# PSUM given out as three pairs of banks, each read by one VectorE operation, in a mixer kernel on one core

## The chip, the cores and the metric

The kernel runs on one core of a Trainium2 chip. The metric is the device time of one execution in microseconds, the median of several runs. TensorE (PE) multiplies, with its weight loads shown as PEld; VectorE (DVE) and ScalarE (ACT) read TensorE's results out of PSUM; GpSimd (POOL) and SyncE (SP) mostly issue DMAs. [...]

## What is computed

```python
# x: (8, 4096, 192), softmax weights over 7 taps for each of 8 heads
w = softmax(weight)                                    # (8 heads, 7 taps)
x = causal convolution of x with w along the sequence  # (8, 4096, 192)
xt = x.transpose(0, 2, 1)
h = np.maximum(xt @ w_tok1, 0.0) @ w_tok2              # mixes the 4096 tokens through 256
u = x + h.transpose(0, 2, 1)
h2 = np.maximum(u @ w_ch1, 0.0) @ w_ch2                # mixes the 192 channels through 1536
return (u + h2).astype(np.float32)
```

Weights arrive as float64, are decoded on the chip, and split into a high and a low fp32r part, so that most products are made of three matmuls: high by high, high by low, low by high.

## The kernel before

The eight batches are worked in five groups: 0, 1, then 2 and 3, 4 and 5, 6 and 7 (`GROUPS`). For each group stage 1 makes the convolution (taps on VectorE, line 718) and the first token product (line 821 for one batch, 825 to 827 for two) into two PSUM banks of their own, `ps_a`. Then the tokens are walked in eight tiles of 512 (`q`), and each tile is 4 blocks of 128 tokens (`j`, `TJ = 4`).

For a tile and a batch the order on TensorE is this. `channel1` (line 1154) multiplies the tile with `w_ch1`: six turns `p`, each of 18 matmuls into two banks; ScalarE writes the ReLU `hh` of each bank (line 1212) and VectorE the remainder `hl` (line 1213), which also is the last read of the bank. In the last batch of a group's tile, `mix2` then makes the next tile's second token product (lines 980 and 981 for one batch, 983 to 985 for two), a bank for each `j`, and VectorE adds it to `u` (lines 989, 990, or 1000 with a VectorE transpose on line 1001). `channel2` (lines 1247 and 1248) multiplies by `w_ch2`, a bank for each `j`, and VectorE makes two adds for each `j` into `osb` (lines 1253 and 1254). It is called for the first half (`j` = 0, 1) and for the second (`j` = 2, 3). Between the halves the next tile is turned so that channels lie on partitions. In the first group, and in the first turns of the second, that is `transposed()`: eight TensorE transposes into two banks (line 1040), copies on ScalarE and a subtraction on VectorE (line 1043). In later turns it is done by VectorE's 32x32 transposes, 16 DMAs (`blocks_sent`, line 1071) and copies (`parted`, lines 1100 to 1107), under channel2. From the third group on the tiles of the first batch use `channel2_halves` (line 1230), two banks for each `j`, and in some turns `mix2_halves` (line 1015).

All of these take their banks from one pool, `ps_x`, of six buffers of a bank each. The pool gives them out in turn: the seventh request gets the first bank again, and its first matmul waits until all that read or wrote that buffer are done.

Convolution, decoding and the first token product of the coming groups run in the background. `Background` holds queues of items, each with a cost in ns. After each piece of foreground work `bg.fg(pe, dve, after)` advances a planned TensorE clock and pops items until the planned VectorE clock is `after` ahead of TensorE's, then charges `dve` for the foreground's own VectorE work. So these numbers set in which order VectorE's instructions stand. `pop` lets the VectorE clock lag at most 3 us behind before it counts an item.

Of the kernel before, what the change touches and what calls it, by code (L numbers as in the profile page):

```python
# [139 lines left out]
def conv_mixer_kernel(ctx: ExitStack, tc: tile.TileContext, x, weight, w_tok1, w_tok2, w_ch1, w_ch2, out):  # L140
# [6 lines left out]
    P = 128  # L147
# [239 lines left out]
    def mix1_done(gi, accs):  # L387
        n = len(GROUPS[gi]) * D
        for kc in range(KC):
            a = accs[kc][:, :n]  # L390
            nc.scalar.activation(out=h1[:, kc, 0, :n], in_=a, func=AF.Relu)
            nc.vector.scalar_tensor_tensor(
                out=h1[:, kc, 1, :n], in0=a, scalar=0.0, in1=f32(h1[:, kc, 0, :n]), op0=ALU.max, op1=ALU.subtract
            )
# [15 lines left out]
    def stage1_first(pe, p0, p1, pd, late, load_u, load_next, after, thirds, hooks):  # L410
# [90 lines left out]
        def keep_busy(n):  # L501
            ps = ps_x.tile([P, TT], F32, name="ps_x")
            for k in range(n):
                nc.tensor.transpose(out=ps[:, k % TJ * P:(k % TJ + 1) * P], in_=ident, identity=ident)

        def make_band(between):
# [16 lines left out]
            for hs in halves:  # L523
                if hs.start:
                    between()
                ps = ps_x.tile([P, P // BC, H2, BC], F32, name="ps_x")
# [3 lines left out]
                ps = ps_x.tile([P, 2, 2, BC], F32, name="ps_x")  # L530
# [7 lines left out]
        def conv_mm(m):  # L538
# [424 lines left out]
    def mix2(gi, q, t2, u, turned=None):  # L963
# [9 lines left out]
        for j in range(TJ):  # L973
            ps = ps_x.tile([P, TT], F32, name="ps_x")
# [11 lines left out]
            bg.fg(570 if nb == 1 else 1040, 660 if nb == 1 else 600, 200)  # L986
            if nb == 1:
                two, one = flat(u)[:, j, 0], flat(u)[:, j, 1]
                nc.vector.tensor_tensor(out=one, in0=ps[:, D:2 * D], in1=one, op=ALU.add)
                nc.vector.tensor_tensor(out=two, in0=ps[:, :D], in1=one, op=ALU.add)  # L990
                if turned is not None:
                    nc.vector.transpose(
                        out=by_rows(turned, 1)[:, :, :, j * QB:(j + 1) * QB],
                        in_=two.rearrange("p (c q e) -> p c q e", c=ND, e=QB),
                    )
                    bg.dve += 380
            else:
                uj = u[:, j]
                v = ps[:, :n].rearrange("p (b c d) -> p c b d", b=nb, d=D2)
                nc.vector.tensor_tensor(out=uj, in0=v, in1=uj, op=ALU.add)  # L1000
                nc.vector.transpose(
                    out=by_rows(turned, nb)[:, :, :, j * QB:(j + 1) * QB],
                    in_=uj.rearrange("p c b d -> p c (b d)").rearrange("p c (q e) -> p c q e", e=QB),
                )
                bg.dve += 580

    def mix2_halves(gi, t2, u, turned, j):
        nb = len(GROUPS[gi])
        n = nb * D
        pss = [ps_x.tile([P, TT], F32, name="ps_x") for _ in range(2)]  # L1010
# [9 lines left out]
        uj = u[:, j]  # L1020
        for ps in pss:
            v = ps[:, :n].rearrange("p (b c d) -> p c b d", b=nb, d=D2)
            nc.vector.tensor_tensor(out=uj, in0=v, in1=uj, op=ALU.add)
        nc.vector.transpose(
            out=by_rows(turned, nb)[:, :, :, j * QB:(j + 1) * QB],
            in_=uj.rearrange("p c b d -> p c (b d)").rearrange("p c (q e) -> p c q e", e=QB),
# [5 lines left out]
    def transposed(u):  # L1032
# [4 lines left out]
        for c, (cs, rs) in enumerate(((slice(0, P), slice(0, P)), (slice(P, D), low))):  # L1037
            ps = ps_x.tile([P, TT], F32, name="ps_x")
# [88 lines left out]
    def first_mix(t2, between=None, u=None):  # L1127
        u = first["u"][1] if u is None else u
        for j in range(TJ):
            ps = ps_x.tile([P, TT], F32, name="ps_x")  # L1130
# [5 lines left out]
            bg.fg(650, 350, 200)  # L1136
            two, one = flat(u)[:, j, 0], flat(u)[:, j, 1]
            nc.vector.tensor_tensor(out=two, in0=ps[:, :D], in1=one, op=ALU.add)
# [8 lines left out]
    def channel1_mm(t, p, prods=PRODS, pss=None, last=False):  # L1147

        a, z = pss is None, last or prods[-1] == PRODS[-1]
        pss = pss or [ps_x.tile([P, TT], F32, name="ps_x") for _ in range(2)]  # L1150
        for n, (w, v, c) in enumerate(prods):
            for h, ps in enumerate(pss):
# [375 lines left out]
```

## Time and profile before

| | |
|---|---|
| median of 3 runs | 2005.45 us (2005.21 to 2005.59) |
| the profiled execution | 2005.44 us, span 2003.7 us |
| busy, share of the span | PE 1998.3 us (100%), PEld 1851.7 (92%), DVE 1500.3 (75%), ACT 779.9 (39%), POOL 205.8 (10%) |
| granted TensorE clock | 1.0 |

The span is the time from the first to the last instruction, and 1.7 us lie around it. In the rows of the groups by line, the columns are the line, engine, operation, what it writes and reads with the shapes and the count, then busy us and mean ns of one, then the idle time of the engine ahead of it and what ended it. Rows of the timeline and of the chain begin with the start in us and the length in us. A matmul's end is modelled and matmuls overlap, so their starts are the better clock.

### The profile page before, as it was taken

Reading aid. Unit: us, or ns where it says so; the run is one execution under the profiler, and the core shown is the slowest. Engines: PE = TensorE matmul, PEld = TensorE weight load, DVE = VectorE, ACT = ScalarE, POOL = GpSimd, SP = SyncE. Lnnn points to the kernel's source line nnn. Section 1 sums busy time; section 2 is a strip of 40 time slices with the busy share of each in tenths; the row PEclk is TensorE's granted clock in tenths of the full one; section 3 lists DMA queues with packets and bytes.
Section 4 is the critical chain, followed back from the end, with each engine's and each line's share of the span. In section 5 each row is a group of like instructions: output and inputs, shape, how many; then the busy total and the mean of one; then the engine's idle time right before and its main releaser. Section 6 shows DMA issues by size and latency. Waiting matters only on the chain.

```text
span 2003.7 us, 44785 instructions
## 1 busy us (share of the span) xinstructions
PE 1998.3 (100%) x18652; PEld 1851.7 (92%) x18652; DVE 1500.3 (75%) x2998; ACT 779.9 (39%) x1292; POOL 205.8 (10%) x385
## 2 busy tenths in 40 slices
PE   9999999999999999999999999999999999999999
PEld 9899999999999999998999999999999999999998
DVE  8889989999759998848975789556666666666664
ACT  5777534534343443423433433323233322333322
POOL 0000000011211101111011010101111101011110
PEclk9999999999999999999999999999999999999999
DMA  9947445556465457514664434433223233233310
GB/s 308 317 137 226 151 129 171 177 161 195 159 179 144 134 160 201 158 51 115 165 172 110 126 101 143 136 88 85 78 49 85 72 84 77 71 85 86 85 49 17
DMA packets 270361, 262.21 MB, mean 131 GB/s; under 512 B 189136, under 2 KB 218192, under 8 KB 270160
## 3 DMA queue, kind: packets, MB, share of 16 engines
q1 hardware_dynamic: 248432, 185.27, 32.6%
q0 software_dynamic: 21728, 74.08, 12.1%
q8 instruction: 148, 2.42, 0.5%
q14 instruction: 53, 0.43, 0.1%
HBM read 146.31 MB, written 71.30 MB: 109 GB/s over the span
## 4 chain that ended last, share of the span: by engine, by line
PE 93%; DVE 4%; ACT 1%; DMA 1%; issue 0%; SPq 0%; DVEq 0%; ACTq 0%
PE ps_x L1154 38%; PE ps_x L1230 23%; PE ps_x L1247 12%; PE ps_x L1248 5%; PE ps_x L1015 2%; PE ps_a L825 2%; PE ps_a L826 2%; PE ps_a L827 2%; DVE xc L718 2%; PE ps_a L476 1%; PE ps_x L983 1%; PE ps_x L980 1%; PE ps_x L985 1%; PE ps_x L984 1%; PE ps_a L821 1%; DMA early_raw<-in_moe_w_tok_dram 1%
## 5 line engine op out<-in xcount | busy, mean ns | idle before, releaser
L1212 ACT ACTIVATE hh<-ps_x 128x512 fp32r<-128x512 f32 x744 | 404.0, 596 | 844.1 <-PE ps_x L1154 844.0
L1213 DVE SCALAR_TENSOR_TENSOR hl<-ps_x,hh 128x512 fp32r<-128x512 f32 x744 | 476.9, 685 | 188.1 <-ACT hh L1212 186.8
L1230 PE MATMUL ps_x<-w,hh 64*128 64x384 f32 x3360 | 481.5, 355 | 0.0
L1230 PE MATMUL ps_x<-w,hl 64*128 64x192 f32 x3360 | 423.0, 247 | 0.0
L718 DVE SCALAR_TENSOR_TENSOR xc<-raw,cw,xc 128x384 f32<-128x384 f32 (+1 forms) x768 | 387.9, 561 | 7.8 <-ACT xc L716 7.8
L1247 PE MATMUL ps_x<-w,hh 128*128 128x384 f32 x1284 | 369.6, 359 | 0.0
L1154 PE MATMUL ps_x<-other,w_hi 64*128 64x512 f32 x1296 | 337.4, 388 | 0.0
L1154 PE MATMUL ps_x<-own_hi,w_hi 64*128 64x512 f32 x1440 | 333.3, 392 | 0.5 <-DVE osb L1238 0.3
L1154 PE MATMUL ps_x<-own_hi,w_lo 64*128 64x512 f32 x1440 | 327.3, 387 | 0.0
L1154 PE MATMUL ps_x<-own_lo,w_hi 64*128 64x512 f32 x1440 | 327.0, 387 | 0.0
L1230 PEld LDWEIGHTS ps_x<-w,hl 64*128 64x128 f32 x3360 | 323.6, 188 | 0.9
L1248 PE MATMUL ps_x<-w,hl 128*128 128x192 f32 x1284 | 321.4, 250 | 0.0
L1230 PEld LDWEIGHTS ps_x<-w,hh 64*128 64x128 f32 x3360 | 317.8, 184 | 0.9
L1154 PEld LDWEIGHTS ps_x<-other,w_hi 64*128 64x128 f32 x1296 | 235.5, 184 | 22.9 <-issue 0.4
L1248 PEld LDWEIGHTS ps_x<-w,hl 128*128 128x128 f32 x1284 | 245.1, 191 | 0.0
L1154 PEld LDWEIGHTS ps_x<-own_lo,w_hi 64*128 64x128 f32 x1440 | 218.1, 184 | 25.9 <-ACT own_lo L1046 0.4
L1154 PEld LDWEIGHTS ps_x<-own_hi,w_lo 64*128 64x128 f32 x1440 | 218.2, 184 | 25.8
L1247 PEld LDWEIGHTS ps_x<-w,hh 128*128 128x128 f32 x1284 | 241.1, 188 | 0.4 <-DVE hl L1213 0.4
L1154 PEld LDWEIGHTS ps_x<-own_hi,w_hi 64*128 64x128 f32 x1440 | 212.3, 184 | 31.4 <-issue 4.6
L1154 PE MATMUL ps_x<-other,w_lo 64*128 64x512 f32 x648 | 181.5, 386 | 0.0
L1238 DVE TENSOR_TENSOR osb<-ps_x,osb 128x192 f32<-128x192 f32 x420 | 150.2, 358 | 25.0 <-DVE osb L1238 0.5
L1236 DVE TENSOR_TENSOR osb<-ps_x,u 128x192 f32<-128x192 f32 x140 | 49.8, 355 | 135.8 <-PE ps_x L1230 135.8
(185 smaller groups left out, 2426.3 us busy)
## 6 DMA issues: line engine op xcount, KB each, us to landing
raw<-in_x_dram SPq DMA_DIRECT2D x56, 672.0 KB, 7.4
t<-t2d SPq DMA_DIRECT2D x64, 512.0 KB, 5.5
u<-xcd SPq DMA_DIRECT2D x62, 384.0 KB, 7.4
xcd<-xc POOLq DMA_DIRECT2D x28, 768.0 KB, 8.3
t<-t1p SPq DMA_DIRECT2D x32, 512.0 KB, 4.5
out_dram<-osb POOLq DMA_DIRECT2D x34, 384.0 KB, 3.2
out_dram<-osb SPq DMA_DIRECT2D x29, 384.0 KB, 2.8
t2d<-stage SPq DMA_DIRECT2D x16, 512.0 KB, 4.8
```

Of the source, the lines that this page charges most:

```text
L718: nc.vector.scalar_tensor_tensor(out=dst, in0=src, scalar=cw[:, h, k:k + 1], in1=dst, op0=ALU.mult, op1=ALU.add)
L825: nc.tensor.matmul(out=ps, lhsT=wh, rhs=xh, start=a, stop=False)
L826: nc.tensor.matmul(out=ps, lhsT=wh, rhs=xl, start=False, stop=False)
L827: nc.tensor.matmul(out=ps, lhsT=wl, rhs=xh, start=False, stop=z)
L1154: nc.tensor.matmul(out=ps, lhsT=w1[w][rows, t[h][2][c], p * P:(p + 1) * P], rhs=t[h][v][rows, c], start=a and n == 0, stop=z and n == len( ...
L1212: nc.scalar.activation(out=h["hh", f], in_=ps, func=AF.Relu)
L1213: nc.vector.scalar_tensor_tensor(out=h["hl", f], in0=ps, scalar=0.0, in1=f32(h["hh", f]), op0=ALU.max, op1=ALU.subtract)
L1230: nc.tensor.matmul(out=ps[:, :m], lhsT=h[part, f][ks, ts], rhs=w2[ks, f, :m], start=n == 0 and part == "hh", stop=z and part == "hl",)
L1236: nc.vector.tensor_tensor(out=rows(osb[:, j]), in0=rows(pss[0][:, :D]), in1=tokens(u, i)[:, j], op=ALU.add)
L1238: nc.vector.tensor_tensor(out=osb[:, j], in0=v, in1=osb[:, j], op=ALU.add)
L1247: nc.tensor.matmul(out=ps[:, :2 * D], lhsT=h["hh", f][:, ts], rhs=w2[:, f, :], start=n == 0, stop=False)
L1248: nc.tensor.matmul(out=ps[:, :D], lhsT=h["hl", f][:, ts], rhs=w2[:, f, :D], start=False, stop=z)
```

## The change

The pool becomes three buffers of two banks. `banks()` takes a pair, `bank()` takes a pair and uses the first half only. Where work filled two banks, one VectorE operation now reads both: in `channel1` the remainder of both halves (but for the last `p`, which has one operation for each bank), in `mix2` and `channel2` the adds of two `j`, in `first_mix` and `first_channel2` the same for the first tiles. The transposes on VectorE stay one for each `j`. `mix1_done` writes `h1` in the order of `u`, so that an add over two batches is contiguous, and makes its remainder by batch. `transposed` and `keep_busy` take `bank()`. The charges to the planner change with it: for a pair of `j`, 0 after the first and 1120 after the second in place of 660 each (`mix2` for one batch and `channel2`), 930 in place of 600 each (`mix2` for two), 1250 in place of 1300 in `channel1`.

```diff
-    ps_x = ctx.enter_context(tc.tile_pool(name="ps_x", bufs=6, space=bass.MemoryType.PSUM))
+    ps_x = ctx.enter_context(tc.tile_pool(name="ps_x", bufs=3, space=bass.MemoryType.PSUM))
+    def banks():
+        return ps_x.tile([P, 2, TT], F32, name="ps_x")
+    def bank():
+        return banks()[:, 0]
...
     def mix2(gi, q, t2, u, turned=None):
...
-            ps = ps_x.tile([P, TT], F32, name="ps_x")
+            if j % 2 == 0:
+                pair = banks()
+            ps = pair[:, j % 2]
...
-                nc.vector.tensor_tensor(out=one, in0=ps[:, D:2 * D], in1=one, op=ALU.add)
-                nc.vector.tensor_tensor(out=two, in0=ps[:, :D], in1=one, op=ALU.add)
+                nc.vector.tensor_tensor(out=one, in0=pair[:, :, D:2 * D], in1=one, op=ALU.add)
+                nc.vector.tensor_tensor(out=two, in0=pair[:, :, :D], in1=one, op=ALU.add)
...
-                nc.vector.tensor_tensor(out=uj, in0=v, in1=uj, op=ALU.add)
-                nc.vector.transpose(
+                nc.vector.tensor_tensor(out=uj, in0=pair[:, :, :n], in1=uj, op=ALU.add)
+                for k in range(2):
+                    nc.vector.transpose(
...
     def transposed(u):
...
-            ps = ps_x.tile([P, TT], F32, name="ps_x")
+            ps = bank()
...
     def channel1(t, hold):
...
-            bg.fg(2040 if p else 2400, 1300)
-            for f, ps in pss:
-                nc.scalar.activation(out=h["hh", f], in_=ps, func=AF.Relu)
+            bg.fg(2040 if p else 2400, 1250)
+            hh, hl = parts["hh", p], parts["hl", p]
+            for k in range(2):
+                nc.scalar.activation(out=hh[:, k], in_=pss[:, k], func=AF.Relu)
+            for ks in [slice(0, 1), slice(1, 2)] if p == NP - 1 else [slice(0, 2)]:
                 nc.vector.scalar_tensor_tensor(
-                    out=h["hl", f], in0=ps, scalar=0.0, in1=f32(h["hh", f]), op0=ALU.max, op1=ALU.subtract
+                    out=hl[:, ks], in0=pss[:, ks], scalar=0.0, in1=f32(hh[:, ks]), op0=ALU.max, op1=ALU.subtract
                 )
...
     def channel2(i, h, u, osb, js, at=None):
-        for j in js:
+        pair, last = banks(), js[-1]
+        for k, j in enumerate(js):
...
-            ps = ps_x.tile([P, TT], F32, name="ps_x")
+            ps = pair[:, k]
...
-                    bg.fg(1140, 660 if z else 0, 200)
+                    bg.fg(1140, (0, 660, 1120)[len(js)] if z and j == last else 0, 200)
...
-            nc.vector.tensor_tensor(out=rows(osb[:, j]), in0=rows(ps[:, :D]), in1=tokens(u, i)[:, j], op=ALU.add)
-            nc.vector.tensor_tensor(out=osb[:, j], in0=ps[:, D:2 * D], in1=osb[:, j], op=ALU.add)
+        pair, js = pair[:, :len(js)], slice(js[0], last + 1)
+        nc.vector.tensor_tensor(
+            out=osb[:, js].rearrange("p j (c d) -> p j c d", d=D2),
+            in0=pair[:, :, :D].rearrange("p j (c d) -> p j c d", d=D2), in1=tokens(u, i)[:, js], op=ALU.add,
+        )
+        nc.vector.tensor_tensor(out=osb[:, js], in0=pair[:, :, D:2 * D], in1=osb[:, js], op=ALU.add)
```

Two places show what becomes of the order. The first is TensorE in the third tile of the first group, where channel2's first half ends, the eight transposes follow, and channel2's second half begins. The number behind `ps_x` tells one buffer request from another; the brackets name the engine whose count is waited for. Before, lines 1247 and 1248 are channel2 and 1040 the transposes:

```order
L1247 MATMUL ps_x_1466<-w2_1167,hh8_1222 128x384
L1248 MATMUL ps_x_1466<-w2_1167,hl8_1223 128x192
L1040 MATMUL ps_x_1508<-ident_71,u_1216 128x128 [waits DVE_49,PE_49]
L1040 MATMUL ps_x_1508<-ident_71,u_1216 128x128 [waits DVE_49] x3
L1040 MATMUL ps_x_1515<-ident_71,u_1216 64x128 [waits PE_49]
L1040 MATMUL ps_x_1515<-ident_71,u_1216 64x128 x3
L1247 MATMUL ps_x_1526<-w2_1167,hh0_1218 128x384 [waits PE_49]
L1248 MATMUL ps_x_1526<-w2_1167,hl0_1219 128x192
```

The same place after the change, where channel2 is on lines 1282 and 1283 and the transposes on 1057:

```order
L1282 MATMUL ps_x_1381<-w2_1131,hh8_1186 128x384
L1283 MATMUL ps_x_1381<-w2_1131,hl8_1187 128x192
L1057 MATMUL ps_x_1455<-ident_71,u_1180 128x128 [waits DVE_49,PE_49]
L1057 MATMUL ps_x_1455<-ident_71,u_1180 128x128
L1057 MATMUL ps_x_1455<-ident_71,u_1180 128x128 [waits DVE_49]
L1057 MATMUL ps_x_1455<-ident_71,u_1180 128x128
L1057 MATMUL ps_x_1462<-ident_71,u_1180 64x128 [waits PE_49]
L1057 MATMUL ps_x_1462<-ident_71,u_1180 64x128 x3
L1282 MATMUL ps_x_1473<-w2_1131,hh0_1182 128x384 [waits DVE_49,PE_49]
L1283 MATMUL ps_x_1473<-w2_1131,hl0_1183 128x192
```

The second half's first matmul now also waits for VectorE: by the count it waits for, for the second add that reads `ps_x_1381`, the pair of the first half. The same wait stands in all eight turns that have a whole channel2 around `transposed()`.

The second place is VectorE in the sixth tile of the first group, from mix2's adds (before lines 989 and 990, after 1003 and 1004) to channel2's first-half adds; `xc` is written by taps of the next group's convolution. After the change:

```order
L1246 SCALAR_TENSOR_TENSOR hl8_2345<-ps_x_2475,hh8_2344 128x512
L727 SCALAR_TENSOR_TENSOR xc1_2517<-raw0_2286,cw_70,xc1_2517 128x8x24 [waits DVE_49] x10
L1003 TENSOR_TENSOR u_2338<-ps_x_2503,u_2338 128x2x192 [waits DMAHW4_49,PE_49]
L1004 TENSOR_TENSOR u_2338<-ps_x_2503,u_2338 128x2x192 [waits DVE_49]
L727 SCALAR_TENSOR_TENSOR xc1_2517<-raw0_2286,cw_70,xc1_2517 128x8x24 [waits DVE_49] x6
L1003 TENSOR_TENSOR u_2338<-ps_x_2547,u_2338 128x2x192 [waits PE_49]
L1004 TENSOR_TENSOR u_2338<-ps_x_2547,u_2338 128x2x192 [waits DVE_49]
L727 SCALAR_TENSOR_TENSOR xc1_2517<-raw1_2495,cw_70,xc1_2517 128x8x24 [waits DVE_49] x10
L1289 TENSOR_TENSOR osb_2502<-ps_x_2584,u_1951 128x384 [waits DMASW6_49,PE_49]
L1293 TENSOR_TENSOR osb_2502<-ps_x_2584,osb_2502 128x384 [waits DVE_49]
```

Rows of one or two taps beside these are left out; with them there are 12 taps ahead of the first pair of adds, 8 between the pairs and 18 ahead of line 1289, where before four pairs of shorter adds and channel2's adds for `j` = 0 stood among them. TensorE's mixing matmuls of this turn (line 821 before), which stood inside the half and ahead of, among and behind the transposes, now all stand ahead of channel2's first half.

More of the change, by code (lines that the diff above doesn't have):

```diff
@@ L525, in make_band @@
                     between()
-                ps = ps_x.tile([P, P // BC, H2, BC], F32, name="ps_x")
+                ps = bank().rearrange("p (b h c) -> p b h c", h=H2, c=BC)
                 for b0 in range(P // BC):
@@ L1009, in mix2_halves @@
         n = nb * D
-        pss = [ps_x.tile([P, TT], F32, name="ps_x") for _ in range(2)]
+        pair = banks()
+        pss = pair[:, 0], pair[:, 1]
         prods = [(kc, r, v) for kc in range(KC) for r, v in ((0, 0), (0, 1), (1, 0))]
@@ L1037, in transposed @@
         for c, (cs, rs) in enumerate(((slice(0, P), slice(0, P)), (slice(P, D), low))):
-            ps = ps_x.tile([P, TT], F32, name="ps_x")
+            ps = bank()
             for j in range(TJ):
@@ L1129, in first_mix @@
         for j in range(TJ):
-            ps = ps_x.tile([P, TT], F32, name="ps_x")
+            if j % 2 == 0:
+                pair = banks()
+            ps = pair[:, j % 2]
             for kc in range(KC):
@@ L1135, in first_mix @@
                 )
-            bg.fg(650, 350, 200)
-            two, one = flat(u)[:, j, 0], flat(u)[:, j, 1]
-            nc.vector.tensor_tensor(out=two, in0=ps[:, :D], in1=one, op=ALU.add)
+            bg.fg(650, 560 if j % 2 else 0, 200)
+            if j % 2:
+                two, one = (flat(u)[:, j - 1:j + 1, t] for t in range(2))
+                nc.vector.tensor_tensor(out=two, in0=pair[:, :, :D], in1=one, op=ALU.add)
             if between and j == 0:
@@ L1166, in first_two @@
             done = [channel1_mm(first["abc"][0], p, prods, pss) for p, pss in enumerate(done)]
-        for f, ps in (v for d in done for v in d):
-            nc.scalar.activation(out=first["h"][:, f], in_=ps, func=AF.Relu)
+        for p, pss in enumerate(done):
+            for h in range(2):
+                nc.scalar.activation(out=first["h"][:, p + h * NP], in_=pss[:, h], func=AF.Relu)
         bg.fg(4080, 0)
@@ L1174, in first_channel1 @@
         bg.fg(2040, 0)
-        for f, ps in pss:
-            nc.scalar.activation(out=first["h"][:, f], in_=ps, func=AF.Relu)
+        for h in range(2):
+            nc.scalar.activation(out=first["h"][:, p + h * NP], in_=pss[:, h], func=AF.Relu)
     def first_channel2(u, osb, steps):
@@ L1180, in first_channel2 @@
         n = NF // 3
-        for t, j in steps:
+        for k, (t, j) in enumerate(steps):
             a, z = t == 0, t == 2
-            if a:
-                pss[j] = ps_x.tile([P, TT], F32, name="ps_x")
+            both = j < 2 and (0, 0) in steps and (0, 1) in steps[:2]
+            if a and not (both and j):
+                pss[j] = banks()
+                if both:
+                    pss[1] = pss[0]
+            ps = pss[j][:, j if both else 0]
             for f in range(t * n, (t + 1) * n):
                 nc.tensor.matmul(
-                    out=pss[j][:, :D], lhsT=first["h"][:, f, j * P:(j + 1) * P], rhs=w2f[:, f], start=f == 0,
+                    out=ps[:, :D], lhsT=first["h"][:, f, j * P:(j + 1) * P], rhs=w2f[:, f], start=f == 0,
                     stop=f == NF - 1,
                 )
-            bg.fg(1280, 270 if z else 0, 200)
+            z = z and (j or not both)
+            bg.fg(1280, (560 if both else 270) if z else 0, 200)
             if z:
+                js = slice(0, 2) if both else slice(j, j + 1)
                 nc.vector.tensor_tensor(
-                    out=rows(osb[:, j]), in0=rows(pss[j][:, :D]), in1=tokens(u, 0)[:, j], op=ALU.add
+                    out=osb[:, js].rearrange("p j (c d) -> p j c d", d=D2),
+                    in0=pss[j][:, :js.stop - js.start, :D].rearrange("p j (c d) -> p j c d", d=D2),
+                    in1=tokens(u, 0)[:, js], op=ALU.add,
                 )
@@ L1223, in channel2_halves @@
             ts = slice(j * P, (j + 1) * P)
-            pss = [ps_x.tile([P, TT], F32, name="ps_x") for _ in range(2)]
+            pair = banks()
+            pss = pair[:, 0], pair[:, 1]
             for n, f in enumerate(order):
```

74 lines of the change are left out of this document (42 added, 32 removed).

## The prediction

> **What bounds the kernel now.** First the page's span and busy line for TensorE, with its chain of waits:
>
> ```profile
> span 2003.7 us, 44785 instructions
> ...
> PE 1998.3 (100%) x18652; PEld 1851.7 (92%) x18652; DVE 1500.3 (75%) x2998; ACT 779.9 (39%) x1292; POOL 205.8 (10%) x385
> ...
> PE 93%; DVE 4%; ACT 1%; DMA 1%; issue 0%; SPq 0%; DVEq 0%; ACTq 0%
> ```
>
> TensorE is busy from end to end, and 93% of the chain is TensorE's own work. A matmul's end is modelled, so I asked next for the waits of PE (who waited for whom, us in total, times, longest):
>
> ```profile
> PE ps_x L504 <- POOL ident masks.py:199: 1.4, 1, 1.4
> PE ps_x L1154 <- DVE osb L1238: 0.3, 1, 0.3
> PE ps_a L476 <- ACT xc L569: 0.2, 1, 0.2
> ```
>
> That is 1.9 us. Short waits hide under a modelled end, but show on the weight loads. Those that waited for channel1's VectorE operation (L1213, "who waited for it": us, times):
>
> ```profile
> who waited for it (us, times):
>   PEld ps_x L1154: 2.9, 9
>   PEld ps_x L980: 2.9, 8
> ```
>
> So at most 2.9 + 2.9 = 5.8 us of TensorE's time is owed to VectorE's reads of channel1's banks. VectorE is close to full in only one long stretch, the first group's tiles (columns: length, then busy us of PE, PEld, DVE, ACT, POOL):
>
> ```profile
> 120.00:400.00 280.00, 279.79 (x2117) 263.87 (x2114) 256.22 (x583) 160.07 (x260) 16.59 (x25) 1.00 0.53 169
> ```
>
> 256.22/280 is 92%, yet PE lost 0.21 us there by these rows. The matmuls are the same before and after, so a faster VectorE can give back 5.8 us at most; a new wait on PSUM is paid in full. The question is which waits the new rotation makes.
>
> **Fewer and longer VectorE operations.** Durations by shape:
>
> ```profile
> L1213 DVE SCALAR_TENSOR_TENSOR hl<-ps_x,hh 128x512 fp32r<-128x512 f32 x744 | 476.9, 685 | 188.1 <-ACT hh L1212 186.8
> ...
> L1023 DVE TENSOR_TENSOR u<-ps_x,u 128x384 f32<-128x384 f32 x88 | 48.6, 553 | 4.9 <-DVE u L1023 0.5
> ...
> L1254 DVE TENSOR_TENSOR osb<-ps_x,osb 128x192 f32<-128x192 f32 x107 | 38.3, 358 | 3.7
> L1253 DVE TENSOR_TENSOR osb<-ps_x,u 128x192 f32<-128x192 f32 x107 | 37.8, 354 | 68.5 <-PE ps_x L1248 67.9
> ...
> L205 DVE SCALAR_TENSOR_TENSOR t<-dec_raw,t 128x1024 uint32<-128x1024 uint32 x6 | 7.3, 1222 | 0.1
> ...
> L205 DVE SCALAR_TENSOR_TENSOR w2f<-dec_raw,w2f 128x768 uint32<-128x768 uint32 x3 | 2.9, 958 | 0.1
> ```
>
> A tensor_tensor of 2x192 columns should take what 384 columns take, 0.55 us, in place of two of 0.355; a channel1 operation over 1024 columns 1.22 us (the nearest row, 1024 columns from SBUF) in place of two. VectorE loses some tens of us of work over the run. On the path this is worth nothing by itself: it can only shorten the 5.8 us above.
>
> In channel1 a pair comes free in another order. One pair of a late tile (start, length):
>
> ```profile
> 644.96 0.39 PE L1154 MATMUL ps_x<-other,w_hi 64*128 64x512 f32 x1
> ...
> 645.15 1.09 ACT L1212 ACTIVATE hh<-ps_x 128x512 fp32r<-128x512 f32 x2 [2.57 <-PE ps_x L1154]
> ...
> 645.78 1.29 DVE L1213 SCALAR_TENSOR_TENSOR hl<-ps_x,hh 128x512 fp32r<-128x512 f32 x2
> ```
>
> Before, VectorE starts after the first ReLU (645.78) and is done at 647.07. Now it waits for both (646.24) and ends 1.22 us later, at about 647.5: 0.4 us later than before. Whatever VectorE holds queued behind this operation waits with it, for 0.5 us. TensorE needs those banks three pairs on, after two more pairs of work. From the chain:
>
> ```profile
> 612.58 12.27 PE ps_x L1154 x108
> ```
>
> 12.27/6 = 2.04 us for a pair, so the matmuls that reuse the banks start 4.1 us after the old ones ended (at about 649.1), 1.6 us after the new release. Covered; where VectorE is behind, it is not ReLU that it waits for, and its two operations cost 1.22 in place of 1.29 us. I put this at nothing, and keep 0.5 us in each of ten tiles (5 us) as a bound.
>
> **The new wait.** Six banks gave out one at a time; now three pairs do. In the tiles that use transposed() one turn takes six pairs in channel1, two in mix2, one for channel2's first half, two (one bank of each used) in transposed(), one for the second half. With three buffers, the second half gets the pair that the first half just filled, and must wait for both adds of it (the order in the section before shows that wait). Only the eight transposes stand between. Before, the second half took a bank untouched since long before. This happens in eight turns: the six with q from 2 to 7 of the first group, and two of the second. The first of them, before (PE, then VectorE):
>
> ```profile
> 132.50 0.44 PE L980 MATMUL ps_x<-h,t2s 128*128 128x384 f32 x1
> ...
> 134.88 0.36 PE L1247 MATMUL ps_x<-w,hh 128*128 128x384 f32 x1
> ...
> 141.62 0.25 PE L1248 MATMUL ps_x<-w,hl 128*128 128x192 f32 x1
> 141.71 1.03 PE L1040 MATMUL ps_x<-ident,u 128*128 128x128 f32 x8
> ...
> 142.50 0.42 PE L1247 MATMUL ps_x<-w,hh 128*128 128x384 f32 x1
> ...
> 143.43 0.35 DVE L1253 TENSOR_TENSOR osb<-ps_x,u 128x192 f32<-128x192 f32 x1
> 143.82 0.36 DVE L1254 TENSOR_TENSOR osb<-ps_x,osb 128x192 f32<-128x192 f32 x1
> ```
>
> The half's last matmul ends at 141.87, and the second half starts at 142.50, 0.63 us later. VectorE's add starts at 143.43: it is 1.56 us behind. The same spot in a turn where VectorE is idle:
>
> ```profile
> 311.34 0.25 PE L1248 MATMUL ps_x<-w,hl 128*128 128x192 f32 x1
> ...
> 311.67 0.35 DVE L1253 TENSOR_TENSOR osb<-ps_x,u 128x192 f32<-128x192 f32 x1
> ```
>
> 311.67 is 0.08 us after the matmul's end at 311.59. Two adds of 384 columns, 0.03 us apart as L1253 and L1254 are, take 0.55 + 0.03 + 0.55 = 1.13 us. Even with an idle VectorE the pair is free 0.08 + 1.13 = 1.2 us after the half's end, against 0.63: a stall of 0.6 us, and what VectorE is behind comes on top. Forced part: 8 x 0.6 = 4.8 us.
>
> How far VectorE is behind in the new order: in the first turn the two adds of j = 0 (0.74 us) no longer stand ahead, and mix2's adds are shorter, while channel1's last operations end some 0.5 us later; 1.56 - 0.74 + 0.4 is 1.2 us. The worst is the turn at 241:
>
> ```profile
> 239.21 6.01 DVE L718 SCALAR_TENSOR_TENSOR xc<-raw,cw,xc 128x192 f32<-128x192 f32 x18
> ...
> 242.46 0.25 PE L1248 MATMUL ps_x<-w,hl 128*128 128x192 f32 x1
> 242.55 1.49 PE L821 MATMUL ps_a<-xc,t 128*128 128x192 f32 x8
> ...
> 245.13 0.35 DVE L1253 TENSOR_TENSOR osb<-ps_x,u 128x192 f32<-128x192 f32 x1
> ```
>
> VectorE was 2.4 us behind (245.13 against 242.71), and nobody waited. A tap there takes 6.01/18 = 0.33 us. The new order has 38 taps and two pairs of mix2 adds between channel1's last operation and these adds: 38 x 0.33 + 2 x 1.1 = 14.7 us, from about 2.5 us after channel1's end (both ReLUs to 646.24 as above, then two operations of one bank, 1.29), so 17.2. TensorE's side: mix2 2.4 (132.50 to 134.88), four mixing blocks of eight matmuls, now all ahead of the half, 4 x 1.3 = 5.2 (242.55 to 243.87 is one), the half 6.8 (134.88 to 141.71): 14.4. Behind by 2.8; I take 2.6 with the measured turn. For the other six I take nearly the idle row, 0.5 us in sum. Their bounds are 0 and 1.56 each. Sum of the new wait: 4.8 + 1.2 + 2.6 + 0.5 = 9.1 us.
>
> [...]
>
> **What the stalls give back.** A TensorE that is held up lets VectorE catch up, and two channel1 stages that waited for VectorE's backlog follow directly on such turns (near 155 and near 260 us). The chain ahead of the first of them:
>
> ```profile
> 152.99 2.08 DVE xc L718 x6
> 155.07 1.21 DVE hl L1213 x2
> ...
> 156.32 1.89 PE ps_x L1154 x13
> ```
>
> Six taps stood in front of the operation that frees the banks. Of the 5.8 us I take 1.7 back; bounds 0 and 2.9.
>
> **The transposed copy for later groups.** mix2 now ends with one add of 768 columns (0.96) and two transposes in place of one add and one transpose, so this copy ends some 0.9 us later where VectorE is idle. What follows is a chain of DMAs and copies under channel2, with no slack at one turn:
>
> ```profile
> 1003.83 0.58 DVE L1001 STREAM_TRANSPOSE own_hi<-u 128x384 f32<-128x384 f32 x1
> ...
> 1014.81 1.48 ACT L1105 CAST other<-own_hi 64x1536 fp32r<-64x1536 f32 x1
> ...
> 1016.12 0.50 PE L1154 MATMUL ps_x<-own_hi,w_hi 64*128 64x512 f32 x1
> ```
>
> The cast ends at 1016.29, while channel1 has started. VectorE was behind in that turn already, which hides most of the 0.9; I take 0.3 us, bounds 0 and 2.5. The smaller edits have one answer: mix1_done's operations by batch are a few a group, under a whole channel1; the last tile's adds are single as before; stage 1's keep_busy, bands and convolution take pairs that were read long before.
>
> **Sum.** 9.1 - 1.7 + 0.3 = 7.7 us. The profiled execution took 2005.44 us (span 2003.7), the median is 2005.45: forecast 2013.1 us.
>
> **Rivals.** *VectorE is level at the eight spots.* The planner is told smaller costs and could leave VectorE idle there; then the forced 4.8 alone remains, less up to 2.9: 2007.3 to 2010.2. For it: the row at 311.67. Against it: the row at 245.13, and the queue of 38 taps. It decides below about 1 us of lag in all. Chance 0.15. *VectorE's relief wins.* If grouping frees a nearly full VectorE (92% above), the 5.8 us go and, should the adds come early enough under the transposes, no stall replaces them: 2005.4 - 5.8 = 1999.6. It needs the second add done 0.63 us after the half's end, when one add alone takes 0.55; chance 0.03. [...] *Longer waits everywhere.* VectorE is as far behind as at 143.43 in all other turns, 7 x 1.56 = 10.9 in place of 1.7, or channel1's 5 us come due: 2018 to 2022.3. Against: after such a stall VectorE is level again. Chance 0.17. That the rotation is not as described is excluded by the order.
>
> **How the numbers follow.** The forecast's case (2010.2 to 2018) has 0.65. The range reaches from the first rival's low end, 2007.3, to within the last, 2019.5, and leaves out about 0.03 below and 0.12 above. A measurement tells 0.2% (4.0 us) from no change, so slower means above 2009.5: 0.65 + 0.17 = 0.82; the first rival is nearly all below that, same 0.15; faster 0.03.
>
> **What would show it.** In the new profile, the waits of PE should list channel2's matmul line behind VectorE's second osb add, eight times, 0.6 us and more each, the longest in the turn near 245; PE's busy share in 120 to 400 us should fall by some 3%, and stay as it is after 400. Channel1's operation should take about 1.22 us and the paired adds 0.55. I am wrong if those eight waits are absent or sum to under 4 us, or if PE loses time after 577.

## The result, and the profile after

The changed kernel takes 2021.67 us (median of 5 runs, 2020.09 to 2025.67) against 2005.59 (5 runs, 2005.21 to 2007.62): ratio 1.0083, 95% interval 1.007 to 1.0097. It is slower, as forecast, but by 16 us where 7.7 were forecast, and outside the range.

The page of the profiled execution (2024.02 us, span 2022.3):

```profile
span 2022.3 us, 44055 instructions
...
PE 2002.4 (99%) x18652; PEld 1856.9 (92%) x18652; DVE 1455.9 (72%) x2501; ACT 781.1 (39%) x1292; POOL 205.7 (10%) x385
...
PE 84%; DVE 9%; ACT 2%; DMA 2%; SPq 1%; issue 1%; ACTq 0%; DVEq 0%
```

VectorE has 497 instructions and 44 us of work less, as it should; TensorE's share of the chain fell from 93% to 84%. The operations, by shape, have the forecast durations (1.22 and 0.55 us):

```profile
L1246 DVE SCALAR_TENSOR_TENSOR hl<-ps_x,hh 128x1024 fp32r<-128x1024 f32 x310 | 378.0, 1223 | 201.4 <-ACT hh L1244 201.0
...
L1289 DVE TENSOR_TENSOR osb<-ps_x,u 128x384 f32<-128x384 f32 x53 | 29.4, 554 | 71.9 <-PE ps_x L1283 71.9
```

The waits of PE (us in total, times, longest), the first six rows of nine; before they were 1.9 us in all:

```profile
PE ps_x L1282 <- DVE osb L1293: 8.7, 8, 4.2
PE ps_x L512 <- POOL ident masks.py:199: 1.4, 1, 1.4
PE ps_x L1174 <- ACT own_hi L1098: 1.4, 1, 1.4
PE ps_x L1174 <- DVE hl L1246: 0.9, 2, 0.6
PE ps_x L991 <- DMA t<-t2d: 0.8, 1, 0.8
PE ps_x L1174 <- ACT other L1122: 0.7, 2, 0.4
```

The first row is the new wait, eight times, as announced. The others, but for the 1.4 us on `ident`, which stand in both, are new and were not forecast. Where the time is lost is seen when the same work is put in windows (length, then busy us of PE, PEld, DVE, ACT and POOL with the number of instructions; the granted clock is the third number from the end). Before:

```profile
120.00:388.30 268.30, 268.09 (x2028) 253.59 (x2026) 245.44 (x561) 152.47 (x246) 16.59 (x25) 1.00 0.53 166
388.30:562.80 174.50, 174.50 (x1282) 161.19 (x1280) 149.19 (x298) 66.18 (x119) 30.01 (x56) 1.00 0.58 180
984.40:1122.00 137.60, 137.60 (x1254) 126.33 (x1250) 94.31 (x184) 47.46 (x80) 13.95 (x26) 1.00 0.41 116
```

After:

```profile
120.00:400.00 280.00, 270.41 (x2028) 251.79 (x2026) 235.38 (x455) 152.08 (x247) 16.59 (x25) 0.99 0.50 158
400.00:580.00 180.00, 177.20 (x1280) 162.31 (x1280) 141.66 (x233) 65.44 (x117) 29.99 (x56) 0.99 0.56 175
1000.00:1140.00 140.00, 138.95 (x1253) 129.73 (x1251) 115.51 (x197) 51.42 (x88) 15.37 (x27) 1.00 0.51 145
```

The same 2028 matmuls take 11.7 us longer, the next 1280 take 5.5 us longer, and between 1000 and 1140 a further 2.4 are lost. Between 580 and 1000 some 1.6 came back. From the starts of the matmuls (each gap less the usual one of its form, or less the gap at the same place before) the profiled execution's 18.6 us of span are made up like this; a place is named by the start of its stage:

| where | us |
|---|---|
| the eight waits of channel2's second half: 1.4, 1.0, 0.6, 4.3, 0.6, 0.7, 0.6, 0.8 | +10.0 |
| two stretches of 3.41 us in which TensorE was granted 0.50 of its clock, from 254.9 and 463.1 (see the last section) | +3.2 |
| second group: near 460 (1.4, and 0.6 in the slow matmuls behind it), 496 (0.8), 543 (1.1) | +3.9 |
| channel1 near 1031, 1064 and 1090 | +2.4 |
| the step from mix2 to channel2 near 343 (0.7), and the last add (0.8) | +1.5 |
| channel1 near 119, 150 and 254 no longer waits | -1.9 |
| nor does channel1 near 927 | -1.7 |

That is 17.4; the rest is in gaps too small to tell apart. The half clock is 1.6 us a time: a pair of channel2 matmuls takes 0.535 us in it and 0.285 outside, so 3.41 x (1 - 0.285/0.535).

The longest of the eight waits, near 249, on VectorE and TensorE:

```profile
238.08 4.06 DVE L727 SCALAR_TENSOR_TENSOR xc<-raw,cw,xc 128x192 f32<-128x192 f32 x12 [1.16 <-ACT xc L725]
...
246.81 6.00 DVE L727 SCALAR_TENSOR_TENSOR xc<-raw,cw,xc 128x192 f32<-128x192 f32 x18
252.73 0.55 DVE L1289 TENSOR_TENSOR osb<-ps_x,u 128x384 f32<-128x384 f32 x1
253.31 0.56 DVE L1293 TENSOR_TENSOR osb<-ps_x,osb 128x384 f32<-128x384 f32 x1
...
248.81 1.04 PE L1057 MATMUL ps_x<-ident,u 128*128 128x128 f32 x8
```

The half's last matmul ended near 248.9; 18 taps stood ahead of its adds, and the second half started at 254.01. Ahead of the first of the turn's taps VectorE had also stood idle for 1.16 us, until ScalarE was done. In a turn where VectorE is idle the wait is the forced one; with the modelled end of the transposes 0.46 is shown, by starts 0.62:

```profile
291.03 0.41 PE L1282 MATMUL ps_x<-w,hh 128*128 128x384 f32 x1 [0.46 <-DVE osb L1293]
```

The stall near 460 is of another kind. The chain (start, length; SPq is SyncE issuing DMAs), and the queues of SP and POOL beside it:

```profile
452.97 1.77 SPq L1088
454.74 0.04 issue
454.78 5.72 DMA own_lo<-own_hi
...
460.61 0.63 ACT own_hi L1098
```

```profile
449.24 6.39 SPq L1088 DMA_DIRECT2D own_lo<-own_hi  x8
455.75 5.71 SPq L715 DMA_DIRECT2D raw<-in_x_dram  x2
...
454.32 1.80 POOL L762 DMA_DIRECT2D xcd<-xc  x2
```

The last of the small block copies (48 KB each) took 5.72 us to land, and 2.83 before the change. Two kinds of bulk transfer stand beside it that did not before: stores of the convolution (`xcd`, 768 KB) on POOL, issued around it, and a load of x (672 KB) on SP, issued right behind it. Before the change both came later, after channel1 had begun at 448.15 (the load at 452.53, the stores at 452.76):

```profile
437.38 6.43 SPq L1071 DMA_DIRECT2D own_lo<-own_hi  x8
449.77 0.36 SPq L1272 DMA_DIRECT2D out_dram<-osb  x1
...
452.53 9.30 SPq L706 DMA_DIRECT2D raw<-in_x_dram  x2
...
452.76 1.81 POOL L753 DMA_DIRECT2D xcd<-xc  x2 [1.32 <-DVE xc L718]
```

### The profile page after: what moved, and what is told of

The parts are those of the page before. It is cut to its first block, busy times and chain, and to the rows that moved or that the text cites. A ratio compares the mean times of both kernels' runs of the same rounds, so it can differ in the third digit from the quotient of the medians.

```text
span 2022.3 us, 44055 instructions
## 1 busy us (share of the span) xinstructions
PE 2002.4 (99%) x18652; PEld 1856.9 (92%) x18652; DVE 1455.9 (72%) x2501; ACT 781.1 (39%) x1292; POOL 205.7 (10%) x385
## 4 chain that ended last, share of the span: by engine, by line
PE 84%; DVE 9%; ACT 2%; DMA 2%; SPq 1%; issue 1%; ACTq 0%; DVEq 0%
PE ps_x L1174 35%; PE ps_x L1264 23%; PE ps_x L1282 9%; DVE xc L727 4%; PE ps_x L1283 4%; PE ps_x L1033 2%; DVE hl L1246 2%; SPq L1088 1%; PE ps_a L834 1%; PE ps_a L835 1%; PE ps_a L836 1%; PE ps_x L1211 1%; PE ps_a L484 1%; PE ps_x L994 1%; DMA own_lo<-own_hi 1%
## 5 line engine op out<-in xcount | busy, mean ns | idle before, releaser
L1246 DVE SCALAR_TENSOR_TENSOR hl<-ps_x,hh 128x1024 fp32r<-128x1024 f32 x434 | 457.8, 1069 | 234.1 <-ACT hh L1244 233.6
L1264 PEld LDWEIGHTS ps_x<-w,hl 64*128 64x128 f32 x3360 | 330.8, 188 | 0.8
L1264 PEld LDWEIGHTS ps_x<-w,hh 64*128 64x128 f32 x3360 | 324.9, 184 | 0.8
```

What stands on the lines that cost most here:

```text
L1246: nc.vector.scalar_tensor_tensor(out=hl[:, ks], in0=pss[:, ks], scalar=0.0, in1=f32(hh[:, ks]), op0=ALU.max, op1=ALU.subtract)
L1264: nc.tensor.matmul(out=ps[:, :m], lhsT=h[part, f][ks, ts], rhs=w2[ks, f, :m], start=n == 0 and part == "hh", stop=z and part == "hl",)
```

## Experiments

Each run's time stands beside that of the kernel before, whose medians were 2005.5 to 2005.9.

**One pair for the transposes** (`e1_one_pair`). The changed kernel with, in transposed():

```
+        pair = banks()
-            ps = bank()
+            ps = pair[:, c]
```

The two ScalarE copies then follow both groups of transposes.

> The changed kernel, but transposed() takes both banks of one pair instead of one bank of each of two pairs, so that channel2's second half gets a pair that was read long before. Theory (the rotation is the cause): the eight waits of channel2's second half behind its first half's adds, 10.0 us in the changed kernel's trace, are gone; with them goes the stretch at half clock that follows the longest of them (1.6 us); the two channel1 stages near 155 and 260 lose their 1.2 us to VectorE again; all that is lost after 400 us stays. 2021.7 - 10.0 - 1.6 + 1.2 = 2011. Rival (VectorE's lateness with the longer operations is the cause, wherever the bank comes from): the waits move to the next request, channel1's first pair, and the time stays within 3 us of 2021.7.

2018.54 us (2016.60 to 2020.18), ratio 1.0069 (1.0056 to 1.0083). The eight waits are gone, and so is the half clock behind the longest (the profiled execution's mean granted clock is 1.0, against 0.998 in the changed kernel), yet most of the time is not: the waits of PE now show channel1,

```profile
PE ps_x L1177 <- DVE osb L1296: 3.7, 2, 2.3
PE ps_x L1177 <- DVE hl L1249: 1.5, 3, 1.0
```

with 1.3 us near 128, 2.6 near 160 and 1.8 near 265, by starts. The rival is nearer: a wait for a late VectorE moves to the next pair that is asked for. The rotation decides where it is paid, and only in part whether. A part is the edit's own price: its copies come later, and channel1 near 54 and 88, ahead of the first of the eight turns, takes 1.5 us more than in the changed kernel.

**The old costs** (`e2_old_costs`). The changed kernel with the planner's numbers of the kernel before, for instance

```
-                bg.fg(570, 1120 if j % 2 else 0, 200)
+                bg.fg(570, 660, 200)
...
-                    bg.fg(1140, (0, 660, 1120)[len(js)] if z and j == last else 0, 200)
+                    bg.fg(1140, 660 if z else 0, 200)
```

> The changed kernel with the costs that the planner is told set back, call by call, to the ones of the kernel before; the DMAs stand in the queues of SP and POOL in the order of the kernel before again. Theory (the planner's new order, which moves the loads of x and the taps, causes the losses after 400 us): the stalls near 460 (1.5 us, 0.9 us of slow matmuls behind it and a stretch at half clock, 1.6), 496 (0.8), 543 (1.0) and 1031 to 1090 (2.4 in three) are gone and the 1.7 us near 927 return, while the eight waits stay at 8 to 11 us: 2021.7 - 8.2 + 1.7 = 2015. Rival (the transposed copy of the next group's input, which comes 0.9 us later by its merged add, is the cause): the stalls at 460 and from 1031 to 1090 stay, 2020 to 2022.

2012.2 us (2011.73 to 2012.47), ratio 1.0034 (1.0022 to 1.0047): 9.5 us less. The stalls after 400 are gone to the last one, the one in the channel1 from 927 is back (here from 934), and from 415 to 900 every channel1 starts between 5.9 and 6.3 us later than before. Of the new wait there is left

```profile
PE ps_x L1282 <- DVE osb L1293: 3.7, 7, 0.9
```

by starts 1.05 + 0.66 + 5 x 0.62 = 4.8 us. The eighth, 4.3 us, is gone: in the old order a mixing block stands between half and transposes. The transposed copy, whose adds are still merged, costs nothing.

**The old kernel with the new costs** (`e5_new_costs`). The opposite edit: six single banks, undivided operations, the changed kernel's numbers, in channel2 for instance

```
-                    bg.fg(1140, 660 if z else 0, 200)
+                    bg.fg(1140, (0, 660, 1120)[len(js)] if z and j == js[-1] else 0, 200)
```

> The kernel before, six single banks and all operations undivided, except that the planner is told the costs of the changed kernel, call by call; the DMAs stand in the queues of SP and POOL in the order of the changed kernel. Theory (the planner's new order costs by itself): the stalls near 460 (1.5 us, 0.9 behind it, perhaps 1.6 at half clock), 496 (0.8), 543 (1.0) and 1031 to 1090 (2.4) come, the one near 927 (1.7) goes, and nothing in the turn near 249, whose bank is free long before: 2005.5 + 6 = 2011, between 2009 and 2014. Rival (the new order costs only together with the pairs): 2004 to 2007.

2015.84 us (2013.99 to 2016.33), ratio 1.0047 (1.0035 to 1.006). The new order costs 10 us without a single pair. It loses them partly elsewhere:

```profile
PE ps_x L1154 <- DVE osb L1255: 2.8, 2, 1.5
PE ps_x L980 <- DMA t<-t2d: 2.4, 2, 2.2
```

The first is channel1 near 155 and 260 (1.6 and 1.8 us by starts), which the theory did not foresee. These are the places to which the waits moved with one pair for the transposes, so much of VectorE's lateness there comes from the order, not from the pairs. The second is a load for mix2 that took 11.3 us to land while a store of 768 KB and others ran.

**Which number** (`e9_1250`, `e10_others`). The kernel before with channel1's number alone (1300 to 1250), and with all others but that one:

```
-            bg.fg(2040 if p else 2400, 1300)
+            bg.fg(2040 if p else 2400, 1250)
```

> The kernel before with a single number changed: the planner is told 1250 in place of 1300 for a pair of channel1. The DMA order of SP's queue then differs in a few places only. Theory (what shifts the planner is above all the sums of mix2 and channel2, 800 less a tile and told at every second step; channel1's 300 a tile matter less): 2005 to 2009. Rival (it is channel1's number): 2011 to 2016, as with all of the new costs (2015.8).

> The kernel before with all of the planner's new costs but channel1's (which stays 1300). Theory (the sums of mix2 and channel2 shift the planner): stalls as with all new costs, near 155 and 260 in channel1, at the wait for the mixing operand near 533, 2010 to 2016. Rival (channel1's number does it): 2005 to 2008.

2006.19 us, ratio 1.0002 (0.9993 to 1.001), and 2022.03 us, ratio 1.0082 (1.0068 to 1.0095). So it is the numbers other than channel1's (mix2's, channel2's and those of the first tiles), as expected, but by more than all numbers together: in this order TensorE waits for ScalarE's casts of other tiles.

```profile
PE ps_x L1154 <- ACT own_hi L1100: 2.8, 1, 2.8
PE ps_x L1154 <- ACT own_hi L1081: 1.9, 1, 1.9
PE ps_x L1154 <- ACT other L1105: 1.8, 1, 1.8
```

The costs do not add up: each order has collisions of its own. The second of these rows bears on the stall near 460. The last block copy there was issued at 513.91 and took 4.76 us to land, with stores of the convolution beside it and no load of x (SP issues its next transfer at 523.41):

```profile
513.25 0.92 POOL L753 DMA_DIRECT2D xcd<-xc  x1
514.80 0.90 POOL L753 DMA_DIRECT2D xcd<-xc  x1 [0.63 <-issue]
```

So the stores alone can go with a late copy.

**The load moved back** (`e12_hold`). The changed kernel with the load of x near 460 held until the turn's store is issued; the two stores of the convolution on POOL move behind it too, from 454.32 to 461.27:

```
+                        if not pairs:
+                            bg.hold()
                         other = blocks_sent(z, len(GROUPS[nxt[0]]), sp, "other")
...
+                    if by_blocks and not pairs:
+                        bg.release()
```

> The changed kernel with two transfers moved by one place in their queues: in the second group's turns, loads of x and stores of the convolution that the planner puts between the block copies and the store of the tile's output are held until that store has been issued. On SP this moves one pair of loads of x (672 KB, at 455.75 in the changed kernel's trace), on POOL one store; nothing else moves. Theory (the new order puts this bulk load beside the eight small block copies, which then land in 5.7 us in place of 2.6 to 3.1): the stall near 460, the slow matmuls behind it and the stretch at half clock near 463 go, 1.5 + 0.9 + 1.6 us: 2017.5 to 2019. Rival (the block copies are late because VectorE made the transposed copy late): 2021 to 2022.

2028.01 us (2027.08 to 2028.80), ratio 1.0109 (1.0093 to 1.0126): 6 us more, where 3 to 4 less were expected. At the place itself the theory holds. The longest of the block copies takes 4.4 us to land in place of 5.7, ScalarE's cast starts at 457.28 in place of 460.61, and there is no stall near 460. As load and stores moved together, the run doesn't tell which of them had held the copy up.

```profile
457.28 1.66 ACT L1098 CAST own_hi<-own_lo 128x512 fp32r<-128x512 f32 x3 [14.32 <-DMA own_lo<-own_hi]
...
461.98 7.40 SPq L715 DMA_DIRECT2D raw<-in_x_dram  x2
469.47 3.92 SPq L943 DMA_DIRECT2D t<-t2d  x2
```

But now the load stands in SP's queue ahead of the one for mix2's own operand, `t`, which was issued at 465.30 in the changed kernel. Its two transfers land 7.35 and 5.26 us after they were issued, at 476.82 and 478.19, and TensorE stands idle for them:

```profile
476.96 0.66 PE L991 MATMUL ps_x<-h,t 128*128 128x384 f32 x1 [4.71 <-DVE xc L727]
...
478.23 0.69 PE L991 MATMUL ps_x<-h,t 128*128 128x384 f32 x1 [0.46 <-DMA t<-t2d]
```

The first row names a tap on VectorE, which ended within 0.02 us of the landing at 476.82. But no tap writes what this matmul reads, VectorE had done with the matmul's pair by 470.75 (channel1's fourth turn, three pairs before), and the second row waits for the other half of the same load. So it is the load that TensorE waited for.

**The rotation without the pairs** (`e3_skip_banks`). The kernel before; transposed() passes over two more banks:

```
-            ps = ps_x.tile([P, TT], F32, name="ps_x")
+            ps = [ps_x.tile([P, TT], F32, name="ps_x") for _ in range(2)][0]
```

> The kernel before, with six single banks and undivided operations, except that transposed() takes two more banks, which nobody uses: each request then gives the bank that the pairs' rotation would give. Theory (it is the pair as a unit that makes the wait, not how far the rotation has come): channel2's j = 2 waits only for the adds of j = 0, which were made 3.4 us earlier, so there are at most two short waits (near 141 and 245, where VectorE is 1.6 and 2.4 us behind), under 1 us in all: 2005 to 2007. Rival (the rotation alone costs the eight waits): 8 x 0.2 us from the undivided adds of j = 1 and the lateness of VectorE near 141 and 245 on top, 2009 to 2012.

2005.85 us, ratio 1.0004 (0.9995 to 1.0013). The theory holds: with single banks the same rotation is free.

**All three mended** (`e4_all_three`). Old costs, one pair in transposed(), and in channel2_last

```
-        pair = banks()
-        both, one = pair[:, 0], pair[:, 1]
+        both, one = bank(), bank()
```

> The changed kernel with transposed() in one pair, the planner told the old costs, and the last tile's two products in a pair each instead of one. Theory: with the first two the losses of the changed kernel are gone, with the third the last add no longer waits for the second product (0.8 us at the end). What is left is the kernel before with longer VectorE operations: 2005.6, plus 0 to 1.5 us for the later release in the two channel1 stages near 155 and 260 and in the one near 927: 2005 to 2008. Rival (VectorE's relief is worth something once the waits are gone): 2000 to 2004. Rival (merging costs by itself, channel1's later release or the later copy): 2009 to 2014.

2011.21 us (2010.69 to 2011.48), ratio 1.0029 (1.0018 to 1.0041). My theory fell: only 1.0 us less than with the old costs alone, of which 0.8 is the last add. Nearly all of the 4.8 us went to channel1, above all in the first group, where its stages near 55, 88 and 119 take 2.4 us more than in the kernel before (0.7 with the old costs alone):

```profile
PE ps_x L1177 <- DVE hl L1249: 2.6, 3, 1.2
```

Three runs ask what these 5.7 us are. First the release of a pair.

**Both ReLUs first** (`e8_relu_first`), in the kernel before:

```
+            pss = list(pss)
             for f, ps in pss:
                 nc.scalar.activation(out=h["hh", f], in_=ps, func=AF.Relu)
+            for f, ps in pss:
                 nc.vector.scalar_tensor_tensor(
```

> The kernel before, with one thing moved: in channel1 both ReLUs of a pair are issued ahead of both VectorE operations, so each of these waits, as the merged one does, until both ReLUs are done; banks come free about 0.45 us later (646.9 and 647.5 in place of 646.5 and 647.1 at the pair near 645). Theory (the later release that the prediction put at nothing is what is left of the loss when rotation, costs and tail are mended): channel1's stalls in the first 400 us grow by 3 to 6 us, 2009 to 2011. Rival (the later release is covered, and what is left comes from the pair as the unit in which PSUM is given out): 2005 to 2007.

2006.22 us, ratio 1.0003 (0.9994 to 1.0012). The later release is covered, as the prediction had it.

**One ReLU** (`e11_relu_one`), in the kernel with all three mended:

```
-            for k in range(2):
-                nc.scalar.activation(out=hh[:, k], in_=pss[:, k], func=AF.Relu)
+            nc.scalar.activation(out=hh, in_=pss, func=AF.Relu)
```

> The kernel with all three mended, and channel1's two ReLUs of a pair made one ScalarE operation of 1024 columns, so that the merged VectorE operation starts as soon as that ends. Two ReLUs take 1.09 us end to end and one alone 0.59; one of 1024 columns should take some 0.95 to 1.05, so the pair comes free about 0.1 us earlier. Theory (channel1's stalls in the first 400 us hang on the release): 0.5 to 1.5 us less than 2011.2. Rival (they hang on taps queued in front): 2010.7 to 2011.7.

2011.22 us, no change. One ReLU takes 1.03 us and two took 1.09, so the pair came free only some 0.06 us sooner. This is too little to show whether the release is the limit in the mended kernel.

**The late adds without pairs** (`e13_deferred`). The kernel before with both ReLUs first and its undivided adds in the changed kernel's places, in channel2

```
+            made.append((j, ps))
+        for j, ps in made:
             nc.vector.tensor_tensor(out=rows(osb[:, j]), in0=rows(ps[:, :D]), in1=tokens(u, i)[:, j], op=ALU.add)
```

and likewise in mix2.

> The kernel before, six single banks and the old costs, with its undivided VectorE operations put where the changed kernel has the merged ones: in channel1 both ReLUs first; in mix2 and channel2 the adds of j = 0 wait until j = 1 is computed, and those of 2 until 3. Theory (what is left of the loss with old costs comes from a pair being one unit of PSUM, which is free only when both halves are read): it stays near the kernel before, 2005.5 to 2007.5. Rival (the adds come late, whatever holds the banks): the stalls of the kernel with all three mended, 2009 to 2012.

2005.26 us, ratio 0.9995 (0.9986 to 1.0004). Late adds are free with single banks. So what is left goes with the pair as the unit that PSUM is given out in, and with two things that this run leaves as they were: the mended transposed(), whose copies come later (TensorE waits 0.5 us for one of them near 58 in the mended kernel), and the adds of the first tiles. How the 5.7 us are shared among these was not separated.

**The operations apart in pairs** (`e6_apart`). The mended kernel with channel1's two VectorE operations each behind its own ReLU:

```
             for k in range(2):
+                ks = slice(k, k + 1)
                 nc.scalar.activation(out=hh[:, k], in_=pss[:, k], func=AF.Relu)
-            for ks in [slice(0, 1), slice(1, 2)] if p == NP - 1 else [slice(0, 2)]:
                 nc.vector.scalar_tensor_tensor(
```

> The kernel of the run before with all three mended (one pair in transposed(), the old costs, the last tile's products apart), and channel1's VectorE operation undone on top: two of 512 columns, each behind its own ReLU, as in the kernel before. Theory (the merged operation releases a pair 0.4 to 0.5 us later, the term put at nothing): channel1's stalls in the first 400 us, which are some 4 us above those of the kernel before, lose more than half: 2007 to 2009. Rival (three buffers of a pair are too few for VectorE's backlog, merged or not): they stay, 2010.5 to 2012.

2112.58 us, ratio 1.0531 (1.0516 to 1.0545): it doesn't answer the question. The second ReLU now waits for VectorE's operation on the first half, 372 times:

```profile
ACT hh L1248 <- DVE hl L1249: 404.0, 372, 5.2
```

In the kernel before no ReLU waits for VectorE, with `hh` in the same tiles. So in this program, where a pair is one tile, readers of its two halves on different engines are put in order.

**Work in the longest wait** (`e7_fill`). The changed kernel, with transposed()'s last four transposes made eight times in the turn near 249, giving the same values:

```
+            turns.append(c)
-            for j in range(TJ):
+            for j in [*range(TJ)] * (1 + 7 * (len(turns) == 14)):
                 nc.tensor.transpose(out=ps[rs, j * P:(j + 1) * P], in_=flat(u)[:, j, 0, cs], identity=ident)
```

> The changed kernel with the last four transposes of transposed() made eight times in the turn near 249, the seven more giving the same values: 28 x 0.109 = 3.05 us of TensorE work inside its wait of 4.3 us. Theory (half a clock follows a stretch in which TensorE mostly idled): the wait still ends when VectorE's adds end, the stretch at half clock behind it is gone, and channel1 near 262 starts 1.6 us sooner; the other stretch, near 463, stays; 2020, against 2021.7. Rival (the half clock has another cause): it stays where it is, 2021.7.

2019.37 us (2017.72 to 2021.45), ratio 1.0067 (1.0054 to 1.0081). The rows of TensorE:

```profile
248.04 4.09 PE L1060 MATMUL ps_x<-ident,u 128*128 128x128 f32 x36
253.22 0.41 PE L1285 MATMUL ps_x<-w,hh 128*128 128x384 f32 x1 [1.09 <-DVE osb L1296]
```

The second half starts 5.18 us after the first transpose (5.20 in the changed kernel), and channel1 12.16 us after it in place of 13.85: the half clock behind this wait is gone, 1.7 us (the pairs behind it start 0.29 us apart, 0.53 in the changed kernel). In this execution the stall near 460 didn't come, but a longer one near 537; the execution's mean granted clock was 0.999, so some time at less than the full clock was left in it.

## Why the prediction was wrong, step by step

*The bound* was right: TensorE pays for each new wait, and VectorE's 44 us bought next to nothing.

*The new wait* was right in place, number and cause: 10.0 us against 9.1. The forced 0.6 is 0.62 in every level turn. The turn at 141 cost 1.4 (forecast 1.8), the one near 249 4.3 (forecast 3.2, without VectorE's idle 1.16 us). That one is a wait of the planner's order as much as of the rotation: with the old costs it is zero.

*What the stalls give back*: 1.9 us against 1.7, 1.4 of it in the two channel1 stages named and 0.5 in the one near 119. The 1.7 near 927, which I had not counted, belong to the order: they are gained with single banks and the new costs too, and lost again with the old costs.

*The transposed copy*: 0 in place of 0.3. *Channel1's later release*: 0, as taken, in single banks. In pairs it is not quite nothing: at the step near 343 channel2 waits for channel1's VectorE operation. All kernels with pairs have such a wait ahead of channel2 (0.4 us and more), and none with single banks has (the kernel before, `e3_skip_banks`, `e5_new_costs`, `e8_relu_first`, `e10_others` and `e13_deferred`). Whether the later release or the pair makes it was not tested.

```profile
PE ps_x L1282 <- DVE hl L1246: 0.6, 1, 0.6
```

*The smaller edits have one answer* was wrong at one place. The last tile's adds are single as before, but channel2_last now holds its two products in one pair, and the first add waits for both. Before, the row read

```profile
1999.38 0.36 DVE L1263 TENSOR_TENSOR osb<-ps_x,u 128x192 f32<-128x192 f32 x1 [1.38 <-PE ps_x L1260]
```

and after

```profile
2018.50 0.36 DVE L1303 TENSOR_TENSOR osb<-ps_x,u 128x192 f32<-128x192 f32 x1 [2.70 <-PE ps_x L1302]
```

that is 0.8 us more at the end, where nothing hides it.

*The step that failed* is the one that isn't in the sum: the planner's new order was costed in one turn, by its 38 taps, and taken as free everywhere else. TensorE's share should "stay as it is after 400", and the sign that I had named, PE losing time after 577, came true. Setting the numbers back brings the change to 2012.2 us, 9.5 less; the numbers alone, in the kernel before, cost 10. In the table this term is most of the 3.9 us of stalls from 460 to 543, of the 2.4 from 1031 to 1090 and of the 3.2 at half clock behind two stalls, with the 1.7 near 927 to the other side. It is the larger part of the 8.6 us that the forecast was short (the table's execution took 2.4 us more than the median); the rest is the new wait (0.9), the step near 343 (0.7) and the last add (0.8). I had looked at where the order moves taps on VectorE, and not at where it moves bulk loads and stores in the queues, although the diff changes the numbers from which their places follow. At the stall near 460 a late small copy beside such transfers is seen; for each of the other stalls the step from order to cost was not taken apart.

That 2012.2 lies so near the forecast is luck: with the old costs the new wait is 4.8 us where the forecast has 9.1, and the last add, the step near 343 and slower first tiles make up for it. The kernel with the rotation mended as well shows that waits move rather than go.

*The rivals*. A level VectorE was excluded by the row near 249; the relief did not win. "Longer waits everywhere" had the time (2018 to 2022.3) but not the cause: the other waits of channel2's second half were 0.6 to 1.4 us, and the waits for channel1's operation 0.6 us at most. Undivided operations cost nothing with single banks (2005.85 us with the same rotation); in pairs, channel1's undivided operations gave 2112.58 us.

## What to carry to other kernels

If a change alters numbers from which an order is planned, compare the DMA queues before and after as well as the engine that the change is about, and time the numbers alone: here they cost 10 us where the change without them cost 7. PSUM given out in larger units cost more here than the rotation alone: a pair is free only when both adds are done, 0.62 us too late eight times, while the same rotation with single banks was free (2005.85 us). A wait that another rotation removed came back in part at the next request, as VectorE was still late. And a transfer that is moved out of one collision can delay the next one in its queue (`t` was issued at 469.47 in place of 465.30): check what stands behind it.

## What the runs showed of the hardware

Half clock after a stall. Four windows of the changed kernel (length, busy us of PE, then the others; the granted clock is the third number from the end):

```profile
251.45:254.86 3.41, 0.85 (x6) 0.88 (x7) 3.38 (x9) 0.75 (x2) 0.15 (x1) 1.00 0.00 0
254.87:258.28 3.41, 3.41 (x15) 3.41 (x14) 3.41 (x12) 3.14 (x5) 0.00 (x0) 0.50 0.01 2
459.67:463.08 3.41, 2.00 (x12) 1.06 (x13) 1.82 (x4) 2.47 (x5) 0.00 (x0) 1.00 0.99 264
463.08:466.49 3.41, 3.41 (x18) 2.67 (x18) 1.92 (x5) 1.53 (x3) 0.56 (x1) 0.50 1.16 324
```

TensorE was busy for 0.85 of 3.41 us, and the next 3.41 us were granted at 0.50; then for 2.00 of 3.41 us, and again the next 3.41 us were granted at 0.50. The starts of the two slow stretches lie 208.21 us apart. From 248.04 to 251.45 TensorE was busy for 1.81 us, less than the 2.00 above, and the next 3.41 us were still granted at 1.00. So half clock behind a stall was seen, but not how much idle time brings it, nor what sets its start and its length. The mean granted clock of the changed kernel's runs is 0.999 in the fastest (2020.09 us) and 0.997 in the slowest (2025.67 us), so the half clock may be a part of why they spread over 5.6 us. It was not tested by itself.
